# Constant products in TensorE's early waits, and seven block products for eight in the last output projection

## The chip, the core and the metric

The kernel runs on one core of a Trainium2 chip. A core has five engines that work at the same time and wait for each other through semaphores: TensorE (PE: matmuls, reads SBUF, writes PSUM), VectorE (DVE), ScalarE (ACT), GpSimd (POOL) and SyncE (SP, which here only issues transfers). The data memory on the core is SBUF; PSUM holds what matmuls write, in eight banks. The metric is the device time of one execution in microseconds (us); lower is better. Times given for a kernel are the median of several executions. A profile is one further execution, recorded instruction by instruction.

## What is computed

Two layers: a causal attention that looks at chosen chunks of keys only, and a gated feed-forward network on its result. Cut to what matters:

```python
# q, k, v: 4 batches, 8 heads, 768 positions, 64 dims
k_min, k_max = min and max of k over each chunk of 32 positions
ub = sum over d of max(q * k_min, q * k_max)          # for each query and each of 24 chunks
top_chunks = the 6 chunks with the largest ub (chunks in the future excluded)
scores = q @ k.T / 8, where key's chunk is in top_chunks and key <= query, else -1e9
attn = softmax(scores);  x = attn @ v                 # then heads side by side: 3072 x 512

gate = 1 / (1 + exp(-(x @ w_gate)))                   # w_gate, w_val: 512 x 1536
val = x @ w_val
out = (gate * val) @ w_out                            # w_out: 1536 x 512, out: 3072 x 512
```

## The kernel before

**Units.** The 24 blocks of 128 tokens are dealt into eight units u0 to u7 of three blocks (384 tokens; u2 has two blocks and one of the first blocks). Unit u0 holds first blocks of three batches, whose attention is short (`first`). For each other unit the kernel prepares keys and queries (`keys_wide`, `queries_wide`, `keys_blocks`, `queries_blocks`), bounds the chunks and picks the largest six (`choose`: `ub`, `mx`, `ap`, `apt`), and attends (`attend`: scores `sc`, exponentials `exp`, the causal cut `cm` on GpSimd, values `pv`; `finish` divides and transposes the result into the unit's x, `xT`).

**Feed-forward.** Units 0 to 3 go through `ffn`: for each of twelve blocks of 128 of the 1536 hidden columns a gate product `g` and a value product `v` (four matmuls of 384 columns each), `tanh` on ScalarE and the gated product `hg` on VectorE, that is (tanh + 1) * val, with the factor 0.5 applied later. Then `project_out` multiplies with w_out: for each of the three token blocks twelve accumulating matmuls of 512 columns in three quarters of four (`o0`, `o1`, `o2`), an eviction with the factor 0.5 (`osb`), and a transfer out.

**Pairs.** Units 4 and 5, and units 6 and 7, go through `ffn_pair`, which treats the pair's gate (and value) matrix as two by two blocks: the two units by the two halves of the hidden columns, and the two halves of the contraction. It takes seven block products for eight. In each of six rounds f, for the gate (g) and the value (v), TensorE runs the products P1 to P7 of two 384-column matmuls each, into three PSUM tiles; ScalarE or VectorE keep three intermediate states (`E0`, `E1`, `E3`), VectorE adds to them (`C0`, `C1`, `C3`), ScalarE takes the `tanh`, and VectorE makes four gated products `hg_u6u7_x_fb` (unit x of the pair, hidden block fb: f or f + 6). Three of the four read the gate and the kept state, both in SBUF; the fourth, unit 0 with block f + 6, reads its value from PSUM. The sums of weights that it needs (`Sg`, `Sv`) and of tokens (`T`) are made on VectorE. After the rounds, `project_out` runs for the two units as for the others; because each token block's twelve matmuls accumulate over the hidden blocks, its quarters may be taken up as soon as four hidden blocks are ready, in the midst of later rounds. Unit 7's last token block is evicted in two parts (384 and 128 columns).

**Order.** All operations are recorded in a plan with their readers and writers; the order in which they are emitted stands in a table written out in the file, `ORDER`. One word of it names an operation, after @ the engine where it has a choice, and after a colon the numbers of the buffers or PSUM banks that it takes. Each engine works through its operations strictly in this order. The weights come by transfers that GpSimd issues from its own queue (`wg0`, `wv0` and so on: the first third of w_gate, of w_val); they stand behind two small copies (`after0`, `after1`) that wait for early transfers. Queries, keys and values are issued by SP in the table's order.

The lines of the profile that matter here: L501 and L502 issue the weights, L520 and L525 first blocks, L940 is `g` and `v`, L971 the output projection, L980 and L981 its evictions, L1049 the products of a pair, L1064 its additions, L1079 its gated products, L577 the difference of chunk maxima and minima (`kcr`), L874 the causal cut, L349 copies on GpSimd.

Of the kernel before, what the change touches and what calls it, by code (L numbers as in the profile page):

```python
# [11 lines left out]
ALU = mybir.AluOpType  # L12
# [82 lines left out]
vf1_1:0 k1_u1:0 ident q3_u1 ident16 epat0:0 kf1_0:0 tri0 epat qf0_0:1 qf1_0 kf0_0 k2_u2:1 kn_u1_1@POOL:1 hkp011@ACT  # L95
hkp000 kf1_1:2 tri qf0_1:3 kf0_1 v10 scm_0:0,1 hkp001@POOL k3_u2 qf1_1 qfT_0:2 vf_0:4 kfT_0:3 kf0_2:5 qf16_0@DVE:2
kf16_0@DVE:3 vf_1:1 kfT_1:4 kn_u2_2@DVE:4 q2_u2 qn_u1_3@DVE:5 hkf0@DVE kT_u1_1:5 ap0 scf_0:1 hkp110 k0_u1 kt_u1_1:0
expf_0_0 kf1_2 kxf1:0 v16_0_0 expf_0_1:2 qf1_2:0 kcr0 hkp101@POOL kf16_1@DVE:6 qfT_1:6 q3_u2 kx0_u1_1 q1_u2 kx1_u1_1:1
qT_u1_3:7 pvf_0_1:2 pvf_0_0:0 qf0_2 hk1_u1_1@POOL rzf_0_1:0 rzf_0_0:1 q0_u2 kxf0 kT_u2_2:1 vc_1 kn_u1_0:1 q0_u1
xf_0_1:0 qf16_1:2 kT_u1_0:4 hkp010 k0_u2 kt_u2_2:1 scm_1:5,3 k3_u1 xf_0_0:1 hk0_u2_2@ACT vf_2:2 kt_u1_0:2 qf_u1_3:0  # L100
kfT_2:2 scf_1:3 k1_u2 kf16_2:5 qfT_2:6 hq0_u1_3@POOL expf_1_0 k2_u1 scm_2:0,7 hk0_u1_1@POOL qf16_2@DVE:4 expf_1_1:1
q2_u1 after0 pvf_1_0:2 kcr_f@POOL kx0_u2_2 after1 hk0_u1_0@ACT q1_u1 pvf_1_1:5 hk1_u1_0 scf_2:3 qn_u1_0:1 xpsf_0_1:6,0
kx1_u1_0 v_0_1:4 kn_u1_3@POOL:2 hkp111@ACT hkf1@DVE wg0 rzf_1_1:0 rzf_1_0:1 xf_1_0:2 qm_u1_3:0 vf1_2:6 kx0_u1_0
xpsf_0_0:3 wv0 vc_2@ACT xf_1_1:0 expf_2_1:2 xTf_0_0 kn_u1_2@DVE:3 expf_2_0 pvf_2_1:2 kn_u2_1:0 qn_u1_1@POOL:4
pvf_2_0:4 kn_u2_0:5 xpsf_1_1:5 kn_u2_3:6 xTf_1_1 xpsf_1_0:3 hk1_u2_2@ACT rzf_2_1:0 rzf_2_0:1 kx1_u2_2:0 kT_u1_3:7
xTf_0_1 qT_u1_0:0 xf_2_1:1 kt_u1_3:1 kx1_u1_3 hk1_u1_3@POOL qf_u1_0 kT_u2_3:5 xTf_1_0 kT_u1_2:1 qn_u2_3@POOL:2 wv1
kx1_u1_2 wg1 kt_u1_2@DVE:0 xf_2_0:0 hk1_u1_2@ACT v11 kx0_u1_3 qT_u1_1:6 wg2 hq1_u1_0 qf_u1_1@DVE xpsf_2_1:2
qm_u1_0@ACT wv2 kx0_u1_2 kT_u2_0:3 xTf_2_1 kT_u2_1:0 kx1_u2_3 qn_u2_2@POOL:1 kx0_u2_3 wo1 kt_u2_3@DVE:2 qT_u2_3:4
kx0_u2_0 hkp100@POOL kx1_u2_0 kcr_u1 kcr1 kx0_u2_1 qn_u2_1@DVE:6 hq0 hq1 ap1 hk0_u1_2 qf_u2_3@DVE:1 xpsf_2_0:7
# [1122 lines left out]
```

## Time and profile before

| | |
|---|---|
| median of 3 runs | 292.14 us (290.18 to 292.30) |
| the profiled execution | 293.76 us |
| its span, first to last instruction | 292.1 us |
| mean clock granted to TensorE | 0.977 of full |
| TensorE (PE) busy | 274.0 us, 94% |
| VectorE (DVE) busy | 239.4 us, 82% |
| ScalarE (ACT) busy | 211.0 us, 72% |
| GpSimd (POOL) busy | 108.1 us, 37% |

The page gives totals, a row of forty slices for each engine, the chain of work that ended last, and groups of like instructions. Matmuls overlap each other, and their ends are modelled, so busy time of TensorE is not work at its peak; the step from one start to the next says more. An engine that is idle costs nothing by itself: it costs where the engine that sets the end waits for it. The granted clock is the share of full speed that TensorE was given in a stretch.

### The profile page before, as it was taken

What the parts mean: (1) busy time and instruction counts of PE and PEld (TensorE: products, weight loads), DVE (VectorE), ACT (ScalarE), POOL (GpSimd) and SP (SyncE); (2) the same over time, 40 slices, a digit from 0 to 9 for tenths busy, and PEclk for the clock granted to TensorE, in tenths of its full rate; (3) what the DMA queues carried; (4) which work ended last, traced back from release to release, by engine and by line L of the source; (5) the groups of instructions that cost most, each with busy time, mean ns of one, the idle gap of its engine ahead of it and who ended that gap; (6) DMA issues with size and microseconds to landing.
All of it is one profiled execution on the core that took longest, in us unless ns stands there. A gap on an engine that the chain in (4) does not pass through costs nothing.

```text
span 292.1 us, 7079 instructions
## 1 busy us (share of the span) xinstructions
PE 274.0 (94%) x2626; PEld 173.6 (59%) x2626; DVE 239.4 (82%) x653; ACT 211.0 (72%) x450; POOL 108.1 (37%) x176
## 2 busy tenths in 40 slices
PE   2578799999999999999999999999999999999994
PEld 1456366665665666656766656966565565655552
DVE  2959675678999998899999998999998446999840
ACT  3296278769677967886878799999985833996422
POOL 7457325445574335494334577450101110000000
PEclk9977599999999999999999999999999999999999
DMA  6999999989989998969800211100000111000013
GB/s 170 242 272 185 210 222 171 180 172 200 214 170 165 185 207 175 187 129 169 211 2 15 61 39 38 38 1 2 1 2 0 74 72 59 16 0 2 1 72 144
DMA packets 123378, 32.69 MB, mean 112 GB/s; under 512 B 111440, under 2 KB 120400, under 8 KB 123344
## 3 DMA queue, kind: packets, MB, share of 16 engines
q1 hardware_dynamic: 118592, 27.53, 44.2%
q0 software_dynamic: 4752, 4.72, 10.3%
q8 instruction: 20, 0.33, 0.5%
q14 instruction: 14, 0.11, 0.1%
HBM read 30.67 MB, written 6.29 MB: 127 GB/s over the span
## 4 chain that ended last, share of the span: by engine, by line
PE 83%; DVE 5%; DMA 5%; SPq 4%; issue 1%; ACT 1%; POOL 1%; DVEq 0%; ACTq 0%
PE o_u L971 19%; PE sc_u L857 11%; PE v_u L940 11%; PE g_u L940 10%; PE pv_u L890 6%; DMA wv<-in_moe_w_val_dram 3%; PE sug_u6u L1049 3%; PE suv_u6u L1049 3%; PE sug_u4u L1049 3%; PE ube_u L796 3%; PE suv_u4u L1049 2%; SPq L525 2%; SPq L536 2%; PE xps_u L917 2%; PE srv_u4u L1049 1%
## 5 line engine op out<-in xcount | busy, mean ns | idle before, releaser
L868 ACT ACTIVATE att_u<-sc_u 128x512 f16<-128x512 f32 (+3 forms) x184 | 90.1, 557 | 21.0 <-PE sc_u L857 17.1
L874 POOL TENSOR_SCALAR_AFFINE_SELECT att_u<-att_u 128x384 f16<-128x384 f16 (+1 forms) x56 | 29.9, 544 | 79.6 <-ACT att_u L868 69.5
L971 PE MATMUL o_u<-wo,hg_u 128*128 128x512 f16 x216 | 54.1, 379 | 0.0
L940 PE MATMUL v_u<-xT_u,wv 128*128 128x384 f16 x192 | 40.4, 334 | 1.8 <-DMA wv<-in_moe_w_val_dram 1.8
L940 PE MATMUL g_u<-xT_u,wg 128*128 128x384 f16 x192 | 39.7, 330 | 0.0
L948 ACT ACTIVATE gate_u<-g_u 128x384 f16<-128x384 f32 x48 | 23.1, 491 | 10.5 <-PE g_u L940 10.2
L971 PEld LDWEIGHTS <-hg_u 128*128 128x128 f16 x216 | 20.0, 98 | 16.8
L952 DVE SCALAR_TENSOR_TENSOR hg_u<-gate_u,v_u 128x384 f16<-128x384 f16 x48 | 25.0, 534 | 5.3 <-PE v_u L940 3.6
L857 PE MATMUL sc_u<-hqe,hke 128*128 128x128 f16 (+2 forms) x220 | 28.0, 243 | 0.0
L857 PE MATMUL sc_u<-hqo,hko 128*128 128x128 f16 (+2 forms) x220 | 27.6, 243 | 0.1
L890 PEld LDWEIGHTS <-att_u 128*128 128x128 f16 x640 | 24.7, 97 | 4.7 <-issue 0.6
L890 PE MATMUL pv_u<-v,att_u 128*128 128x65 f16 x640 | 26.8, 193 | 0.0
L940 PEld LDWEIGHTS <-wv 128*128 128x128 f16 x192 | 18.4, 100 | 12.6 <-DMA wv<-in_moe_w_val_dram 2.1
L940 PEld LDWEIGHTS <-wg 128*128 128x128 f16 x192 | 18.2, 99 | 10.6 <-issue 1.3
L857 PEld LDWEIGHTS <-hko 128*128 128x128 f16 x220 | 16.7, 98 | 8.5 <-issue 1.7
L857 PEld LDWEIGHTS <-hke 128*128 128x128 f16 x220 | 16.9, 98 | 6.4 <-issue 0.3
L971 PE MATMUL o_u<-wo,hgp_u 128*128 128x512 f16 (+1 forms) x72 | 16.4, 370 | 0.0
L562 POOL CAST v<-v 128x512 f16<-128x512 f32 x23 | 14.9, 660 | 0.7 <-DMA v<-in_v_dram 0.3
L909 DVE TENSOR_TENSOR x_u<-pv_u,rz_u 128x384 f16<-128x384 f32 (+1 forms) x28 | 14.5, 528 | 0.4
L981 DVE TENSOR_SCALAR osb_u<-o_u 128x512 f32<-128x512 f32 x10 | 6.8, 681 | 9.8 <-PE o_u L971 9.6
L980 ACT ACTIVATE osb_u<-o_u 128x512 f32<-128x512 f32 (+1 forms) x14 | 8.1, 589 | 8.6 <-PE o_u L971 8.6
L1049 PEld LDWEIGHTS <-Sv 128*128 128x128 f16 x96 | 9.3, 98 | 6.7 <-issue 0.4
(223 smaller groups left out, 602.4 us busy)
## 6 DMA issues: line engine op xcount, KB each, us to landing
v<-in_v_dram SPq DMA_DIRECT2D x23, 256.0 KB, 4.1
out_dram<-osb_u SPq DMA_DIRECT2D x23, 256.0 KB, 2.0
k<-in_k_dram SPq DMA_DIRECT2D x12, 384.0 KB, 5.9
q<-in_q_dram SPq DMA_DIRECT2D x12, 384.0 KB, 5.3
wg<-in_moe_w_gate_dram POOLq DMA_DIRECT2D x3, 512.0 KB, 10.5
wv<-in_moe_w_val_dram POOLq DMA_DIRECT2D x3, 512.0 KB, 9.7
wo<-in_moe_w_out_dram POOLq DMA_DIRECT2D x3, 512.0 KB, 8.8
kf<-in_k_dram SPq DMA_DIRECT2D x8, 128.0 KB, 3.5
```

Of the source, the lines that this page charges most:

```text
L562: plan.add(f"v16_{b}_{ib}", {POOL: pool(H * D)}, lambda e: nc.gpsimd.tensor_copy(v16[b % 2][:, ib, :, 0:D], at(t)), reads=[t], writes=[("v ...
L796: nc.tensor.matmul(at(ub[e_])[32 * p:32 * p + 32, lo - u.s0:hi - u.s0], kcr[par][ROWS[e_], p, m, :], at(src)[ROWS[e_], p, lo:hi], start=(m ...
L857: nc.tensor.matmul(at(t)[:, o:o + 128 * m], hk[b % 2][e_][:, p, 128 * jb:128 * jb + 128], hq[u.side][e_][:, p, 128 * x:128 * (x + m)], sta ...
L868: plan.add(f"exp_{u.name}_{h}_{y}", {ACT: act(n)}, lambda e, t=t, att=att, b0=b0, n=n: nc.scalar.activation(at(att)[:, b0:b0 + n], at(t), ...
L874: nc.gpsimd.affine_select(out=dv, in_=dv, compare_op=ALU.is_ge, fill=0.0, base=0, pattern=[[0, u.m], [1, 128]], channel_multiplier=-1)
L890: nc.tensor.matmul(at(pv)[:, last, x, :], at(att)[:, c:c + 128], v16[b % 2][:, jb, h, :], start=(jb == 0), stop=(jb == ib))
L909: plan.add(f"x_{u.name}_{p}", {DVE: dve(u.t)}, lambda e: nc.vector.tensor_tensor(at(x_).rearrange("p a (e d) -> p e a d", e=2), at(pv)[:, ...
L940: nc.tensor.matmul(at(t), w16[:, c, 128 * fb:128 * fb + 128], at(u.xt)[:, c, :], start=(c == 0), stop=(c == 3))
L948: plan.add(f"tanh_{u.name}_{fb}", {ACT: act(T)}, lambda e, g=g, gate=gate: nc.scalar.activation(at(gate), at(g), AF.Tanh, scale=0.5), read ...
L952: plan.add(f"hg_{u.name}_{fb}", {DVE: dve(T)}, lambda e, w_=w_, gate=gate, hg=hg: nc.vector.scalar_tensor_tensor(at(hg), at(gate), 1.0, at ...
L971: nc.tensor.matmul(at(o), hgs[c][1][1]()[:, 128 * tb:128 * tb + 128], wo16[:, fc, lo:hi], start=(c == 0), stop=(c == NFB - 1))
L1049: nc.tensor.matmul(at(t), left[i](c), right[i](c), start=first and c == 0, stop=c == 1, skip_group_check=not first)
```

## The change

**Constant products.** Thirty matmuls `wm_0` to `wm_29` are added to the plan. Each multiplies the 128x128 identity with itself four times side by side (512 columns) into a PSUM bank that nobody reads. They wait only for the identity and for their bank. The table places them one by one among TensorE's operations: 27 before the first gate product of unit 0, and `wm_7`, `wm_27` and `wm_12` behind it, among unit 0's feed-forward and unit 1's attention.

**The last pair's output projection.** For units 6 and 7 a new function `project_pair` takes the place of two calls of `project_out`. It treats the two units' gated products as two by two blocks (unit, half of the hidden columns) and w_out as two by two blocks (half of the hidden columns, half of the 512 output columns), and forms the four output blocks from seven block products. For this it needs sums:

- `So0` to `So3`, for each of six f: sums of gated products, 128x384 f16 (So0 = unit 7's two halves added, So1 = So0 less unit 6's first half, So2 = unit 6's first half less unit 7's, So3 = unit 6's second half less So1). They may run on VectorE or GpSimd; the table gives 20 of the 24 to GpSimd.
- `To0` to `To3`: differences of blocks of w_out, 128x1536 f16; the table gives all four to GpSimd, To2 in the stage of units 4 and 5, To0 and To1 within the rounds of units 6 and 7, To3 behind them.

Then for each of three token blocks TensorE runs seven products of six 256-column matmuls, into three PSUM tiles; `E0`, `E1`, `E3` keep intermediate states (times 0.5), and `D0` to `D3` write the four output blocks. The sums lie in buffers that held keys and queries of attention.

**The table** is drawn anew: every operation has another place in it, and some have another engine.

The diff without the table, cut to its core:

```diff
+        for f in range(half):
+            a11, a12, a21, a22 = a(0, f), a(0, f + half), a(1, f), a(1, f + half)
...
+            for i, x, op, y, need in ((0, a21, ALU.add, a22, [k21, k22]), (1, lambda f=f: s_(0, f), ALU.subtract, a11, [("so", 0, f), k11]),
+                                      (2, a11, ALU.subtract, a21, [k11, k21]), (3, a12, ALU.subtract, lambda f=f: s_(1, f), [k12, ("so", 1, f)])):
...
+                plan.add(f"So{i}_{tag}_{f}", {DVE: dve(T, 2), POOL: pool(1.6 * T)}, lambda e, i=i, f=f, x=x, op=op, y=y: (
+                    nc.vector if e == DVE else nc.gpsimd).tensor_tensor(s_(i, f), x(), y(), op),
+                    reads=need, writes=[("so", i, f)] + place[room][1], port=True, prio=next_(EV))
...
+        for i, x, op, y, need in ((0, b12, ALU.subtract, b11, []), (1, b22, ALU.subtract, lambda: t_(0), [("to", 0)]),
+                                  (2, b22, ALU.subtract, b12, []), (3, b21, ALU.subtract, lambda: t_(1), [("to", 1)])):
+            plan.add(f"To{i}_{tag}", {DVE: dve(1536, 2), POOL: pool(1.6 * 1536)}, lambda e, i=i, x=x, op=op, y=y: (
+                nc.vector if e == DVE else nc.gpsimd).tensor_tensor(t_(i), x(), y(), op),
+                reads=wos_ + need, writes=[("to", i)] + [(k_, 0, *z) for k_, z in every(0, i // 2)], port=True, prio=next_(EV) - 1)
+        left = {1: lambda f: a(0, f)(), 2: lambda f: a(0, f + half)(), 3: lambda f: s_(3, f), 4: lambda f: a(1, f + half)(),
+                5: lambda f: s_(0, f), 6: lambda f: s_(1, f), 7: lambda f: s_(2, f)}
+        right = {1: lambda f: wo16[:, f, 0:w], 2: lambda f: wo16[:, half + f, 0:w], 3: lambda f: wo16[:, half + f, w:2 * w],
+                 4: lambda f: t_(3, f), 5: lambda f: t_(0, f), 6: lambda f: t_(1, f), 7: lambda f: t_(2, f)}
...
+            op = mul(1, u_, True)
...
+            keep_(0, u_)
+            mul(2, q_, True)
+            done(0, q_)
+            mul(5, r_, True)
+            keep_(3, r_)
+            mul(6, u_, False)
+            keep_(1, u_)
+            mul(3, r_, False)
+            done(1, r_)
+            mul(7, u_, False)
+            done(3, u_)
+            mul(4, u_, False)
+            done(2, u_)
...
+        if ub_ is units[7]:
+            project_pair(ua, ub_, hg, next_)
+            return
         for x, u in ((0, ua), (1, ub_)):
             project_out(u, [(fb, hg[x, fb]) for f in range(half) for fb in (f, f + half)], [], next_)
...
+    for i in range(30):
+        w = ps(f"wm_{i}", "wm", [128, 4, 128])
+        plan.add(f"wm_{i}", pe(512 / 2.4 + 2.4), lambda e, w=w: nc.tensor.matmul(
+            at(w), ident16, ident16.unsqueeze(1).to_broadcast([128, 4, 128]), start=True, stop=True),
+            reads=["ident16"], writes=[w], prio=-2.0 + 0.1 * i)
```

The end of the new table, from the last round on, shows where the sums stand:

```
So3_u6u7_2@POOL E3v_u6u7_5:0 P2v_u6u7_5 C0g_u6u7_5 E1g_u6u7_5:4 P6v_u6u7_5 C0v_u6u7_5 So2_u6u7_3@POOL P7g_u6u7_5
E1v_u6u7_5:3 C3v_u6u7_4 So3_u6u7_3@POOL tanh_u6u7_0_5:1 P7v_u6u7_5 C3g_u6u7_5 P4v_u6u7_4 C3v_u6u7_5 P4g_u6u7_5
hg_u6u7_0_5 P4v_u6u7_5 tanh_u6u7_0_11:1 P3v_u6u7_5 hg_u6u7_0_10 hg_u6u7_0_11 tanh_u6u7_1_11:2 hg_u6u7_1_10 C1g_u6u7_5
P1o_u6u7_1:6,1,2,3,2 P2o_u6u7_0:0 So0_u6u7_4@POOL C1v_u6u7_5 P1o_u6u7_0:7,4,0,1 tanh_u6u7_1_5:3 So1_u6u7_4@POOL
hg_u6u7_1_11 E0o_u6u7_1:6 E0o_u6u7_0:5 hg_u6u7_1_5 So0_u6u7_5 So1_u6u7_5 So3_u6u7_4 So2_u6u7_4 So3_u6u7_5@POOL
```

More of the change, by code (lines that the diff above doesn't have):

```diff
@@ L94 @@
 ORDER = """
[L95 to L109, printed above, removed]
@@ new lines @@
+kn_u2_2@POOL:2 expf_1_1:1 rzf_0_0:0 kt_u1_0@DVE:1 q3_u2 wm_25:0 hq0_u1_3@POOL scm_2:0,5 expf_1_0 xf_0_0:0 k1_u2 wg0
+kx1_u1_0:1 pvf_0_1:6 kf16_2:3 wm_24:1 k3_u2 xpsf_0_0:1,0 kx0_u1_3 wm_5:3 vc_1@ACT qT_u1_1:3 v11 k0_u2 xTf_0_0 wm_6:2
+hk1_u1_0 kT_u2_2:2 qf_u1_1 vf1_3:4 pvf_1_0:7 kcr_f@POOL kT_u1_2:1 vc_2 rzf_1_0:0 kx1_u1_3 scf_2:2 wm_15:3 rzf_0_1:1
+wv0 expf_2_0 wm_10:3 hq1 xf_0_1:1 pvf_1_1:3 expf_2_1:3 xf_1_0:2 pvf_2_0:4 qn_u2_0@POOL:2 wm_19:0 rzf_1_1:0
+kt_u2_2@DVE:2 kn_u2_1:6 wm_17:0 hkp110@POOL xf_1_1:0 pvf_2_1:0 xpsf_1_0:6 rzf_2_0:0 xTf_1_0@ACT xpsf_0_1:7 rzf_2_1:1
```

406 lines of the change are left out of this document (243 added, 163 removed).

## The prediction

> **What bounds the kernel now.** I read the page from the top: engine totals and the slices first.
>
> ```profile
> span 292.1 us, 7079 instructions
> PE 274.0 (94%) x2626; PEld 173.6 (59%) x2626; DVE 239.4 (82%) x653; ACT 211.0 (72%) x450; POOL 108.1 (37%) x176
> PEclk9977599999999999999999999999999999999999
> ```
>
> TensorE (PE) is busy nearly throughout, so shares say little; what counts is which stretch has TensorE at full rate and which does not. So next the busy time by stretches, cut where the work changes (columns: stretch, its length, then busy us and instructions of PE, weight loads, DVE, ACT, POOL, then the granted clock, DMA share, GB/s).
>
> ```profile
> 30.90:36.40 5.50, 5.50 (x36) 2.29 (x44) 3.07 (x9) 0.49 (x1) 0.76 (x2) 0.50 1.39 214
> 187.00:217.00 30.00, 29.88 (x270) 19.47 (x268) 29.51 (x64) 28.15 (x67) 7.10 (x12) 1.00 0.01 2
> 217.00:245.50 28.50, 28.40 (x259) 16.84 (x256) 16.97 (x38) 15.83 (x34) 3.03 (x6) 1.00 0.10 39
> 245.50:280.40 34.90, 34.86 (x207) 19.94 (x206) 31.99 (x66) 23.57 (x55) 0.00 (x0) 1.00 0.04 16
> 280.40:288.30 7.90, 7.87 (x44) 3.69 (x42) 0.69 (x2) 2.18 (x5) 0.00 (x0) 1.00 0.40 155
> 288.30:292.10 3.80, 0.00 (x0) 0.00 (x0) 0.00 (x0) 0.60 (x1) 0.00 (x0) 1.00 0.25 91
> ```
>
> Three things are to be seen. In the first row TensorE works 5.5 us at a clock of 0.50. In the fourth, the last feed-forward pair (units 6 and 7), TensorE is full but VectorE (DVE) has only 2.9 us to spare, and GpSimd (POOL) does nothing at all: 0.00 (x0). In the fifth, after the last gated product, TensorE alone runs for 7.9 us on output projections.
>
> **The start: thirty constant products.** Each is one 128x512 matmul. Twenty-seven stand in TensorE's queue ahead of the first gate product g_u0_0, three behind it.
>
> ```profile
> 13.00:16.40 3.40, 1.53 (x15) 1.16 (x16) 2.13 (x7) 2.06 (x6) 2.15 (x3) 0.98 1.00 249
> 16.40:19.70 3.30, 2.96 (x28) 2.01 (x26) 1.39 (x4) 3.30 (x7) 1.51 (x6) 0.50 0.96 265
> 19.70:23.10 3.40, 1.89 (x29) 1.43 (x26) 3.32 (x12) 3.34 (x8) 2.20 (x5) 1.00 1.07 277
> 26.50:29.90 3.40, 1.59 (x11) 0.86 (x10) 3.40 (x10) 2.75 (x8) 3.36 (x6) 1.00 1.21 188
> 29.90:33.20 3.30, 2.31 (x8) 1.14 (x9) 3.05 (x9) 0.90 (x3) 1.70 (x3) 0.50 1.31 209
> ```
>
> Cut this way the clock follows the stretch before it: after TensorE was busy 1.53 of 3.40 the next stretch has 0.50, after 2.96 of 3.30 it has 1.00, after 1.89 and 1.59 of 3.40 again 0.50, and 2.31 of 3.30 did not yet bring it back. The 5.5 us at half clock from 30.9 therefore hold 2.75 us of loss, and filling the waits can win that much. It wins the full amount only if the wait for the value weights is filled too:
>
> ```profile
> 30.89 1.46 PE L940 MATMUL v_u<-xT_u,wv 128*128 128x384 f16 x4 [1.76 <-DMA wv<-in_moe_w_val_dram]
> 20.11 0.99 POOL wg L501
> 21.15 9.69 DMA wv<-in_moe_w_val_dram
> 7.56 0.51 SPq L520 DMA_DIRECT2D vf<-in_v_dram  x1
> 16.22 0.41 SPq L520 DMA_DIRECT2D vf<-in_v_dram  x1
> vf<-in_v_dram SPq DMA_DIRECT2D x4, 256.0 KB, 3.8
> ```
>
> The first value product started when that transfer landed, 9.69 us after its issue. In the new table GpSimd issues wg0 behind v16_0_0, hkp001 (a 1.46 us copy, row below), kn_u2_2 and hq0_u1_3, and wv0 behind vc_2, which needs the nineteenth and the twenty-sixth load of SP. By the pace of SP before (the two rows are its thirteenth and twenty-seventh load; 3.8 us to landing) I work out some 19 us for wg0 and 21 to 22 for wv0: no earlier landing, so FFN 0 starts at about 31 us as before. Behind g_u0_0 the new order has two more transposes (about 0.4 us each) and three constant products (0.22 each at the full rate below). Start: -2.75 + 0.8 + 0.65 = **-1.3 us**; from -4 (transfer 2.7 us earlier) to +1.5 (clock as before, the added products paid).
>
> **The out-projection of the last pair.** Rates from the chain of waits:
>
> ```profile
> 232.54 1.73 PE o_u L971 x8
> 248.26 0.65 PE sug_u6u L1049 x4
> ```
>
> A 512-wide product takes 0.216 us, a 384-wide one 0.163. Before, units 6 and 7 need the columns of 72 such 512-wide products, 15.6 us. After, 21 block products of six 256-wide matmuls: 126 x 0.109 = 13.7 us (0.109 is half of 0.216). TensorE: **-1.8 us**. But every block product needs the gated products of all six rounds, so none can run inside the pair's stage, where 8.2 us of them ran before. There TensorE now has 82 pair products of two 384-wide matmuls (26.7 us) and one leftover quarter of unit 5 (0.9), VectorE 62 operations. Their pace:
>
> ```profile
> 260.37 0.55 DVE L1064 TENSOR_TENSOR c0g_u6u<-c0g_u6u,sqg_u6u 128x384 f32<-128x384 f32 x1
> 260.84 0.55 DVE L1064 TENSOR_TENSOR c1g_u6u<-c1g_u6u,srg_u6u 128x384 f32<-128x384 f32 x1
> 261.30 0.55 DVE L1064 TENSOR_TENSOR c3g_u6u<-c3g_u6u,sug_u6u 128x384 f32<-128x384 f32 x1
> ```
>
> One starts every 0.47 us: 62 x 0.47 = 29.1. So VectorE is the bound of this stage, without slack, where TensorE was. With 1.5 us at its beginning the last gated product is 30.6 us behind the stage's first product (34.9 before); then the first product on the last sums starts 0.9 later and sixteen products of 0.65 end the kernel: 42.0 against 34.9 + 7.9 = 42.8. With the 0.9 us of unit 5 moved in from before the stage this is the -1.8 again, if nothing else waits. The last eviction is 256 wide in place of 512 (0.60 below): **-0.15 us**.
>
> ```profile
> 286.38 1.89 PE L971 MATMUL o_u<-wo,hgp_u 128*128 128x512 f16 x8
> 288.30 0.60 ACT L980 ACTIVATE osb_u<-o_u 128x512 f32<-128x512 f32 x1 [1.45 <-PE o_u L971]
> ```
>
> **The sums on GpSimd.** The block products need 24 sums of gated products (So, 128x384) and four of weights (To, 128x1536), each of two operands in SBUF; the table gives 20 So and all To to GpSimd. The trace before has no such size there. The nearest rows:
>
> ```profile
> L577 POOL TENSOR_TENSOR kcr<-kx_f,kcr x1: 208/208/208, 17.9 to 17.9; 128x16 f32<-128x16 f32 x1
> L577 POOL TENSOR_TENSOR kcr<-kx_u,kcr x1: 263/263/263, 46.3 to 46.3; 128x32 f32<-128x32 f32 x1
> L577 POOL TENSOR_TENSOR kcr<-kx,kcr x1: 382/382/382, 86.1 to 86.1; 128x96 f32<-128x96 f32 x1
> L349 POOL COPY hke<-kt_u 64x384 f16<-64x384 f16 x1 | 0.5, 501 | 0.0
> L349 POOL COPY hke<-epat 64x1536 f16<-64x1536 f16 x3 | 4.4, 1461 | 0.2
> ```
>
> From 32 to 96 elements an element costs 1.86 ns, from 16 to 96 2.18. Carried on: So 0.92 to 1.01, To 3.06 to 3.51. The copies, with one operand, are the lower end: 0.50 and 1.46. I take 0.97 and 3.3, the rows of the same operation.
>
> What they cost others is in the older pair's rows:
>
> ```profile
> 214.92 0.55 DVE L1079 SCALAR_TENSOR_TENSOR hgp_u<-gate_u4u,c3v_u4u 128x384 f16<-128x384 f16 x1
> 215.39 0.87 DVE L1079 SCALAR_TENSOR_TENSOR hg_u<-gate_u4u,c0v_u4u 128x384 f16<-128x384 f16 x1
> 215.23 0.62 POOL L874 TENSOR_SCALAR_AFFINE_SELECT att_u<-att_u 128x384 f16<-128x384 f16 x1 [7.43 <-ACT att_u L868]
> 207.40 0.83 DVE L1079 SCALAR_TENSOR_TENSOR hgp_u<-gate_u4u,c3v_u4u 128x384 f16<-128x384 f16 x1
> 206.99 0.82 POOL L349 COPY hqo<-apt_u 64x768 f16<-64x768 f16 x1
> ```
>
> A gated product that reads gate and value from SBUF takes 0.55, but 0.87 and 0.83 when GpSimd is at work as it starts; both end 0.41 us after GpSimd's operation (215.85 and 207.81). It waits for the whole of it. In each round of the pair three of the four gated products are of this kind (the fourth reads PSUM). Before, GpSimd idled in this stage. The Trainium skill says the same in "SBUF — State Buffer", section "Who interferes with whom": a VectorE instruction with two SBUF inputs contends with a GpSimd one that reads SBUF, and the later is blocked fully; here the trace agrees (0.87 for 0.55).
>
> I walked the new table's two queues side by side from So0_0 on: 47 VectorE operations, 22 us, against 16 So and two To, 22 us: GpSimd is never ahead, so it is mostly at work when one of the 15 gated products of this kind comes up. To0 starts 1.1 us in and runs to 4.4; hg_1_1 arrives at 1.4 and waits 2.9. To1 runs 8.75 to 12.05; hg_0_2 arrives at 9.2 and waits 2.8. Nine others wait 0.1 to 0.95 for So, 5.2 together. VectorE being the bound, this adds **+10.9 us**; by the copies' prices the same walk gives 2.8. To2 stands in the stage of units 4 and 5, where VectorE is busy 29.51 of 30.00: one gated product arrives some 1.5 us into its 3.3, **+1.8** (0 to 3). So3, So2 and To3 behind the last round end about when their products come up: 0.
>
> The rest of the table, 36 to 187 us, is drawn anew over the same work: 0, give or take 1.5.
>
> **Sum**: -1.3 - 1.8 - 0.15 + 10.9 + 1.8 = +9.45 us. The profiled execution took 293.76 (span 292.1 and 1.66 around it), 1.6 above the median of the runs, 292.14. On that median: 301.6.
>
> **The rivals.**
> *Short sums.* GpSimd takes f16 sums at its copies' price: waits 2.8 + 0.8 instead of 12.7, sum +0.35, 292.5 us. For it: the rows of sums are f32 and small. Against: its copies cost the same in f32 and f16.
> *No meeting*, the one on the faster side: GpSimd's sums do not hold VectorE up, say because the wait falls into time that VectorE spends on the evictions of ScalarE. Place: the last pair; price: the 12.7 away, -3.25, 288.9 us. It decides as soon as all waits are below 3.25, a So of about 0.5. Against it stand the 0.87 and 0.83 and the 29.1 of VectorE over 27.6 of TensorE.
> *The clock falls in the last stage.* With 27.6 us of products in some 41, TensorE is busy 67%; stretches of 47 and 56% above were followed by 0.50, one of 70% did not restore it. Two such stretches at half rate would cost some 4 us: 305.5. The Trainium skill ("TensorE: Matmul & The Clock Gate", Part 1) lets the clock fall only after a whole idle window, about 3.4 us; by that rule this rival is void. Here the trace differs: it fell after 1.89 busy of 3.40.
> *The start does not warm*: the change doesn't do what it says. TensorE still waits for the value weights just before 31 us, and the stretch before is too empty: start +0.65, 303.5.
>
> **How the numbers follow.** Forecast as summed 0.50, no warm start 0.08, falling clock 0.12 (all slower); short sums 0.17; no meeting 0.13. One per cent, 2.9 us, is about what a measurement tells from no change here (the three runs lie 2.1 apart). Slower by more: 0.68, with 0.02 of the slower cases within; within: 0.19; faster: 0.13. The range leaves out no meeting and the far part of the falling clock: 291.5 to 306.5.
>
> **What would show it.** Right: in the last pair, gated products of over 1 us on VectorE that end 0.4 us behind a GpSimd sum; a stage of some 41 us from its first product to the last gated one; So near 1 us, To over 3; clock 1.00 from 31 us. Wrong: gated products at 0.55 throughout, So at 0.5, the last stage under 32 us, or a first value product well ahead of 30 us.

## The result and the profile after

The changed kernel took 302.22 us (median of four runs, 302.0 to 304.58) against 292.06 us for the kernel before on the same chip: a ratio of 1.038, with a 95% interval of 1.031 to 1.045. It is slower by some 10 us. Forecast were 301.6 us.

The page of the changed kernel: span, engine totals, granted TensorE clock in 40 slices. Both profiled executions lie above their kernels' medians, this one (304.58 us, the longest of the four) by 2.4 us and the one before (293.76 us) by 1.7.

```profile
span 302.7 us, 7259 instructions
PE 280.7 (93%) x2698; PEld 178.2 (59%) x2698; DVE 249.7 (83%) x655; ACT 210.7 (70%) x450; POOL 153.4 (51%) x216
PEclk9979999999999999999999999999999999999999
```

GpSimd (POOL) has 45 us more than before. The clock is at full rate from 20 us on, where before the half rate came back at 31 us. The same execution by stretches, with the prediction's columns (length, then busy us and instructions of PE, weight loads, DVE, ACT, POOL, granted clock, DMA share, GB/s), cut where this kernel's work changes:

```profile
30.90:36.40 5.50, 4.72 (x29) 2.65 (x29) 4.74 (x14) 1.38 (x4) 4.65 (x6) 1.00 1.19 189
187.00:217.00 30.00, 28.24 (x268) 18.60 (x266) 29.62 (x60) 27.87 (x65) 10.96 (x12) 1.00 0.01 1
217.00:248.63 31.63, 31.41 (x302) 19.08 (x300) 21.37 (x47) 18.38 (x40) 4.09 (x7) 1.00 0.09 36
248.63:288.21 39.58, 33.76 (x204) 19.66 (x202) 37.72 (x62) 25.26 (x59) 24.12 (x20) 1.00 0.04 13
288.21:299.00 10.79, 10.37 (x92) 8.81 (x91) 6.84 (x17) 1.92 (x5) 5.01 (x3) 1.00 0.26 99
299.00:302.70 3.70, 0.01 (x1) 0.00 (x0) 0.42 (x1) 0.00 (x0) 0.00 (x0) 0.96 0.37 142
```

The last pair's stage (248.63 to the end of the last gated product) takes 39.6 us for 34.9 before. TensorE waits 5.8 us in it and VectorE is busy 37.7 with 62 operations: the bound has passed from TensorE to VectorE. The stretch behind it takes 10.8 us for 7.9. The stage begins 3.1 us later than before (248.63 against 245.49). These three make up the difference of the two spans: 4.7 + 2.9 + 3.1 = 10.7, and 10.6 are measured.

Why VectorE is busy so long is seen in the order of time. First GpSimd's queue, then VectorE's, from the last stage of the changed kernel (start, duration, engine, line, operation, out<-in):

```profile
258.14 0.92 POOL L1026 TENSOR_TENSOR hke<-hgp_u 128x384 f16<-128x384 f16 x1 [15.30 <-DVE hgp_u L1199]
259.01 3.09 POOL L1040 TENSOR_TENSOR hke<-wo 128x1536 f16<-128x1536 f16 x1
...
265.54 3.40 POOL L1040 TENSOR_TENSOR hke<-wo,hke 128x1536 f16<-128x1536 f16 x1
```

```profile
258.98 0.55 DVE L1184 TENSOR_TENSOR c3v_u6u<-c3v_u6u,suv_u6u 128x384 f32<-128x384 f32 x1
259.44 3.08 DVE L1199 SCALAR_TENSOR_TENSOR hgp_u<-gate_u6u,c1v_u6u 128x384 f16<-128x384 f16 x1
...
265.91 0.54 DVE L1184 TENSOR_TENSOR c0g_u6u<-c0g_u6u,sqg_u6u 128x384 f32<-128x384 f32 x1
266.38 2.98 DVE L1199 SCALAR_TENSOR_TENSOR hg_u<-gate_u6u,c0v_u6u 128x384 f16<-128x384 f16 x1
```

To0 runs from 259.01 to 262.10; the gated product that comes up in that time takes 3.08 and ends at 262.52. To1 ends at 268.94; the product that came up at 266.38 ends at 269.36. Both end 0.42 us behind GpSimd. An addition that reads PSUM (265.91), which comes up while To1 runs, takes its usual 0.54.

### The profile page after: what moved, and what is told of

Its sections match the earlier page's. It is cut to its first block, busy times and chain, and to the rows that moved or that the text cites. A ratio compares the mean times of both kernels' runs of the same rounds, so it can differ in the third digit from the quotient of the medians.

```text
span 302.7 us, 7259 instructions
## 1 busy us (share of the span) xinstructions
PE 280.7 (93%) x2698; PEld 178.2 (59%) x2698; DVE 249.7 (83%) x655; ACT 210.7 (70%) x450; POOL 153.4 (51%) x216
## 5 line engine op out<-in xcount | busy, mean ns | idle before, releaser
L979 PE MATMUL o_u<-wo,hg_u 128*128 128x512 f16 x180 | 43.9, 379 | 0.0
L948 PE MATMUL v_u<-xT_u,wv 128*128 128x384 f16 x192 | 39.0, 326 | 0.1
L865 PE MATMUL sc_u<-hqe,hke 128*128 128x128 f16 (+2 forms) x220 | 28.4, 243 | 1.3 <-DVE c1g_u4u L1184 1.3
L865 PE MATMUL sc_u<-hqo,hko 128*128 128x128 f16 (+2 forms) x220 | 28.9, 243 | 0.1
L898 PE MATMUL pv_u<-v,att_u 128*128 128x65 f16 x640 | 27.6, 193 | 0.5 <-DVE c0g_u4u L1184 0.4
L979 PEld LDWEIGHTS <-hg_u 128*128 128x128 f16 x180 | 16.7, 98 | 15.2
L948 PEld LDWEIGHTS <-wv 128*128 128x128 f16 x192 | 18.2, 98 | 10.6 <-issue 0.3
L1026 POOL TENSOR_TENSOR hke<-hgp_u 128x384 f16<-128x384 f16 x5 | 4.6, 914 | 20.7 <-DVE hgp_u L1199 20.7
L1259 PE MATMUL wm<-ident 128*128 128x512 f16 x30 | 12.4, 415 | 0.6
```

The lines of the kernel that those rows point to most:

```text
L865: nc.tensor.matmul(at(t)[:, o:o + 128 * m], hk[b % 2][e_][:, p, 128 * jb:128 * jb + 128], hq[u.side][e_][:, p, 128 * x:128 * (x + m)], sta ...
L898: nc.tensor.matmul(at(pv)[:, last, x, :], at(att)[:, c:c + 128], v16[b % 2][:, jb, h, :], start=(jb == 0), stop=(jb == ib))
L948: nc.tensor.matmul(at(t), w16[:, c, 128 * fb:128 * fb + 128], at(u.xt)[:, c, :], start=(c == 0), stop=(c == 3))
L979: nc.tensor.matmul(at(o), hgs[c][1][1]()[:, 128 * tb:128 * tb + 128], wo16[:, fc, lo:hi], start=(c == 0), stop=(c == NFB - 1))
L1259: plan.add(f"wm_{i}", pe(512 / 2.4 + 2.4), lambda e, w=w: nc.tensor.matmul(at(w), ident16, ident16.unsqueeze(1).to_broadcast([128, 4, 128] ...
```

## The experiments

Each kernel is the changed one with the edit shown. The "held time" counts, over all gated products longer than 0.65 us, what is above 0.54 us for each. In the changed kernel it is 8.2 us in the last stage and 3.1 in the stage of units 4 and 5; in the kernel before it is 0 and 0.6. The ratios are to the kernel before on the same chip. The runs were made on more than one chip, so the difference of two times and the difference of their ratios do not agree to better than about 1 us.

**No constant products, and all sums on VectorE.**

```
-    for i in range(30):
+    for i in range(0):
...
-(thirty words wm_*)
```

> The changed kernel without its thirty constant products, everything else in its order. In its trace a constant product takes 0.43 us from start to start, not the 0.22 of the forecast, so the 27 ahead of the first gate product hold TensorE for 11.6 us and the queue ahead of g_u0_0 is busy nearly without a gap until 34.5 us. Theory A (they fill TensorE's in-order queue and delay its start): g_u0_0 starts at 29 to 32 us, and the time falls by 1.5 to 4 us, to 298 to 300.5 us. Rival (they stand in waits and keep the clock up): g_u0_0 starts where it did, the granted clock falls to 0.5 around it, and the time is the same or rises by up to 3 us, 302 to 305 us.

Measured: 299.16 us, 1.025 (1.017 to 1.033), so some 3 us less than the changed kernel (nearly 4 by the ratios). The start of this kernel, TensorE's queue and GpSimd's issue of the first value weights:

```profile
26.89 0.65 PE L699 MATMUL kT_u<-ident,kn_u 128*128 128x128 f32 x3 [1.33 <-DVE kn_u L351]
27.33 1.48 PE L944 MATMUL g_u<-xT_u,wg 128*128 128x384 f16 x4
29.45 1.37 PE L944 MATMUL v_u<-xT_u,wv 128*128 128x384 f16 x4 [0.64 <-DMA wv<-in_moe_w_val_dram]
```

```profile
20.80 0.80 POOL L506 DMA_DIRECT2D wv<-in_moe_w_val_dram  x1
```

and the same places in the changed kernel:

```profile
33.22 0.44 PE L703 MATMUL qT_u<-ident,qn_u 128*128 128x128 f32 x2
34.12 0.55 PE L703 MATMUL kT_u<-ident,kn_u 128*128 128x128 f32 x3 [0.46 <-DVE kn_u L355]
34.50 0.81 PE L948 MATMUL g_u<-xT_u,wg 128*128 128x384 f16 x4
```

```profile
26.70 0.80 POOL L510 DMA_DIRECT2D wv<-in_moe_w_val_dram  x1
```

Theory A holds: without the constant products the first gate product starts at 27.3 us for 34.5, earlier even than the 29 to 32 expected, though at half rate at first. With them even the issue of the value weights on GpSimd, which has no constant product in its queue, comes 5.9 us later: what TensorE's queue delays, the engines behind it pass on.

```
-So0_u6u7_0@POOL ... To0_u6u7@POOL ...
+So0_u6u7_0@DVE  ... To0_u6u7@DVE  ...      (all 24)
```

> The changed kernel with all 24 sums of the last pair's projection (So and To) on VectorE. Theory A (GpSimd's sums hold VectorE's gated products): the lengthened gated products go, 8.1 us in the last stage and 1.8 in the stage of units 4 and 5; VectorE pays some 14 sums So of 0.27 us and three sums To of 0.9 ahead of its last gated product, 6.4 us. The time is 297.5 us (296 to 299.5), with no gated product over 0.7 us in the last stage. Rival (the loss lies in the projection standing behind the stage and in the table, whichever engine takes the sums): VectorE's stage is only longer by the sums, the time is 302 to 308 us.

Measured: 299.78 us, 1.027 (1.019 to 1.035). This is 0.3 above the range for theory A and 2 below the rival's. No gated product of the last stage is over 0.7 us. The stage of this kernel:

```profile
247.19:285.10 37.91, 33.60 (x202) 19.54 (x201) 36.05 (x82) 25.39 (x59) 0.00 (x0) 1.00 0.04 14
```

GpSimd does nothing in it and VectorE does 82 operations for 62. Forming the sums on VectorE costs the stage nearly what the waits had cost: 37.9 for 39.6 us.

**Three weight sums early on GpSimd; fills in place of sums.**

```
-... To2_u6u7@POOL (stage of units 4, 5) ... To0_u6u7@POOL ... To1_u6u7@POOL (last stage)
+... o0_u4_0 To2_u6u7@POOL ... hg_u4u5_0_11 To0_u6u7@POOL ... sc_u7_5_3 To1_u6u7@POOL
```

> The changed kernel with three of the four weight sums (To0, To1, To2) still on GpSimd, but in the stretch between the stages of the two pairs, where VectorE has few gated products. Theory A: the gated products of 3.08 and 2.98 us in the last stage and the one of 2.36 in the stage of units 4 and 5 become 0.55, which is 6.8 us less on VectorE; the sums So keep their 2.9 us of waits. The time is 295.5 us (294.5 to 297.5). Rival (the stage is lost elsewhere and these waits are covered): 301 to 303 us.

Measured: 300.49 us, 1.030 (1.021 to 1.039). Theory A's number was missed by 5 us. The two queues show why; GpSimd, then VectorE:

```profile
216.43 3.09 POOL L1038 TENSOR_TENSOR hko<-wo 128x1536 f16<-128x1536 f16 x1
219.48 3.41 POOL L1038 TENSOR_TENSOR hke<-wo 128x1536 f16<-128x1536 f16 x1
```

```profile
217.20 2.74 DVE L1197 SCALAR_TENSOR_TENSOR hgp_u<-gate_u4u,c3v_u4u 128x384 f16<-128x384 f16 x1
...
221.32 1.98 DVE L1197 SCALAR_TENSOR_TENSOR hgp_u<-gate_u4u,c1v_u4u 128x384 f16<-128x384 f16 x1
```

A place in the table orders an engine's own queue only. GpSimd had nothing ahead of these sums and ran them from 216 us on, in the middle of the gated products of units 4 and 5. The held time fell from 11.3 to 8.8 us, by 2.5, and the time by 1.7: the theory stands, the edit did not do what I meant.

```
-    nc.gpsimd.tensor_tensor(s_(i, f), x(), y(), op)
+    o, x, y = s_(i, f), x(), y()
+    nc.gpsimd.tensor_tensor(o[:, 0:8], x[:, 0:8], y[:, 0:8], op)
+    for _ in range(2): nc.gpsimd.memset(o[:, 8:T], 0.0)
...
-    nc.gpsimd.tensor_tensor(t_(i), x(), y(), op)
+    for _ in range(2): nc.gpsimd.memset(t_(i), 0.0)
```

> The changed kernel with each sum on GpSimd replaced by work of like length that reads next to nothing: of a sum So only the first 8 columns are formed, and two fills of the whole width follow; a weight sum To becomes two fills of its room. The sums, and so the outputs of the last pair, are left out. Theory A in its narrow form (it is GpSimd's reading of two SBUF tensors that VectorE's gated products wait for): no gated product is over 0.7 us, and the time falls by 8 to 11 us, to 291 to 294 us. Rival (any long work on GpSimd holds them, or they wait for GpSimd's data): gated products stay at 1 to 3 us while the fills run, 300 to 303 us.

Measured: 294.19 us, 1.014 (1.010 to 1.018), 8 us below the changed kernel (7 by the ratios) and 0.2 above the range of theory A. GpSimd, then VectorE, then the stage and the stretch behind it:

```profile
254.24 0.88 POOL L1012 MEMSET hke<- 128x376 f16 x2
255.06 2.81 POOL L1016 MEMSET hke<- 128x1536 f16 x2
```

```profile
255.39 0.55 DVE L1206 SCALAR_TENSOR_TENSOR hgp_u<-gate_u6u,c1v_u6u 128x384 f16<-128x384 f16 x1
...
257.44 0.55 DVE L1206 SCALAR_TENSOR_TENSOR hgp_u<-gate_u6u,c3v_u6u 128x384 f16<-128x384 f16 x1
```

```profile
244.58:276.35 31.77, 31.61 (x197) 19.11 (x196) 29.90 (x62) 24.68 (x59) 21.22 (x52) 1.00 0.04 17
276.35:288.10 11.75, 11.14 (x100) 9.39 (x98) 6.21 (x17) 1.92 (x5) 6.81 (x15) 1.00 0.23 90
```

This is the run that decides. The first gated product is the very one that took 3.08 us in the changed kernel; here it comes up 0.33 us into fills of 2.81 us and takes 0.55. GpSimd is busy 21.2 us of the stage, and not one product of it is held. So neither GpSimd's being at work nor its writing into SBUF holds VectorE; its sums, which read two SBUF tensors, do. In the prediction's rows a causal cut and a copy, which read one, held a product too (0.87 and 0.83). The stage falls from 39.6 to 31.8 us, by 7.8, for 8.2 us of held time in it. The stretch behind it grows by 1.0, from 10.8 to 11.75, so of the 8.2 us held 6.9 are won in the two together. The Trainium skill ("SBUF — State Buffer", section "Who interferes with whom") says of a VectorE instruction with two SBUF inputs that it contends with a GpSimd instruction that reads SBUF and not with one that only writes it: the trace agrees on both halves, 3.08 us beside the sum and 0.55 beside the fill. A fill differs from a sum in its instruction too, so that it is the reading and not the operation is the nearest explanation rather than a proof; that cuts, copies and sums all hold, and fills alone do not, speaks for it.

**The width and the data of a constant product.**

```
-    w = ps(f"wm_{i}", "wm", [128, 4, 128])      ... to_broadcast([128, 4, 128])
+    w = ps(f"wm_{i}", "wm", [128, 2, 128])      ... to_broadcast([128, 2, 128])
```

> The changed kernel with its thirty constant products 256 wide in place of 512. If a constant product's 0.43 us scales with its width, the 27 ahead of g_u0_0 take 5.8 us less of TensorE's queue: theory A (they delay the start) expects g_u0_0 at 28 to 31 us with the clock kept up, and a time 2 to 4 us below the changed kernel's, 298 to 300 us, no worse than without any constant product (299.16). Rival (an instruction costs 0.43 us whatever its width, or the start waits for its transfers): within 1 us of the changed kernel, 301 to 303 us.

```
-    nc.tensor.matmul(at(w), ident16, ident16.unsqueeze(1)...
+    nc.tensor.matmul(at(w), ident16, tri.unsqueeze(1)...
```

> The changed kernel with the mask tile in place of the identity as the moving side of its constant products (weights: the identity, as before); their outputs are read by nobody in either kernel. The two mask products of a block, of the same shape, stand 0.21 us apart in the trace, the constant products 0.43. If the doubled time comes from the identity being both the weights and the moving side, the pitch falls to 0.21 and the time by 1.5 to 4 us, to 298 to 300.5 us. If it belongs to a product that ends its own group in one instruction, the pitch stays 0.43 and the time 301 to 303 us.

Measured: half the width 300.8 us, 1.029 (1.021 to 1.038); the mask tile 303.89 us, 1.041 (1.035 to 1.048). Three constant products in a row in the changed kernel, at half the width, and with the mask tile (three rows from three traces, in this order):

```profile
29.84 1.24 PE L1259 MATMUL wm<-ident 128*128 128x512 f16 x3
```

```profile
28.20 0.92 PE L1258 MATMUL wm<-ident 128*128 128x256 f16 x3
```

```profile
29.61 1.24 PE L1258 MATMUL wm<-tri,ident 128*128 128x512 f16 x3
```

One alone lasts 0.38 at full width and 0.27 at half, so the pitch is (1.24 - 0.38) / 2 = 0.43 and (0.92 - 0.27) / 2 = 0.32 us. Half the width saves 0.11, which is 256 columns at the rate of the out-projections; some 0.21 us of each stay at both widths. Both pitches are the duration and 0.05 us more: what follows a constant product starts when that has ended by the trace (whose ends of products are modelled), while a chain of out-projections overlaps. My first idea, that the identity on both sides doubles it, falls: with the mask tile the pitch is the same. What makes the next product wait stays open. Neither time met its range. With half the width g_u0_0 came at 32.6 us, not at 28 to 31, because the clock in that execution was at 0.50 from 14 to 20 us, and the time lies between the two cases; with the mask tile it is 0.9 above the range, g_u0_0 at 34.3 us after a clock of about 0.7 in the same place.

**The weight sums on VectorE between the stages; no constant products with the fills.**

```
-To0..To3 on GpSimd, in the stages and behind the last
+hg_u4u5_0_11 To0@DVE ... osb_u4_1 To1@DVE ... osb_u4_2 To2@DVE ... hg_u4u5_1_10 To3@DVE
```

> The changed kernel with the four weight sums (To) on VectorE, in the stretch between the two pairs' stages (0.9 us each, where VectorE is busy 21.4 of 31.7 us); the 20 sums So stay on GpSimd. The run with three of them early on GpSimd had its waits moved into the stage of units 4 and 5, since nothing held GpSimd back. Theory A (each us that a gated product is held is lost at the end): the products of 3.08, 2.98 and 2.36 us become 0.55 and no others grow, -6.8 us, with the four sums hidden in VectorE's slack; the time is 295.5 us (294.5 to 297.5). Rival (the stretch has no slack for 3.6 us of VectorE, or only part of the held time counts): 298 to 301 us.

Measured: 297.6 us, 1.020 (1.013 to 1.027), 0.1 above the range for theory A. The two products of 3.08 and 2.98 us are 1.09 and 1.08 here, not 0.55: with the weight sums out of its queue GpSimd forms the sums So earlier, and these now meet the same products. The held time of the last stage is 4.1 us, for 3.2 from the sums So before. Its stage, with GpSimd busy 17.5 us:

```profile
244.57:280.18 35.61, 33.31 (x204) 19.67 (x202) 33.55 (x62) 25.14 (x59) 17.47 (x18) 1.00 0.04 15
```

The stage stands 3.8 us above that with fills: this is the price of the sums So alone.

```
+fills in place of the sums (as above)
-the thirty constant products (as above)
```

> The changed kernel without its constant products and with each sum on GpSimd replaced by fills of like length (of a sum So only 8 columns are formed; the sums, and so the outputs of the last pair, are left out). What stays of the change: the seven block products behind the stage and the redrawn table. If the two effects add, -3.0 and -8.0 us on the changed kernel: 291 us (290 to 292.5), as long as the kernel before. By the forecast's terms without the sums' waits, the time would be 288.5 to 290.5 us: then the effects don't add but the product's saving of 1.8 us is there. Over 292.5 us, the table or the products' place behind the stage costs something of its own.

Measured: 291.76 us, 0.999 (0.995 to 1.002). The two effects add up to the whole of the loss: without the sums' reading and without the constant products the rest of the change, seven block products and a new table, is neither a gain nor a loss to within 0.5%.

**Putting it together.** Six constant products alone; then six, with the weight sums on VectorE and either all or seven of the sums So there as well; then ten, with the weight sums and six sums So on VectorE.

```
-    for i in range(30):
+    for i in (4, 8, 9, 16, 20, 26):
```

> The changed kernel with six of its thirty constant products, those that stand last ahead of g_u0_0 (4, 8, 9, 16, 20, 26). Without any, g_u0_0 came at 27.3 us with TensorE waiting 1.2 and 1.3 us just ahead of it, and the first three feed-forward products ran at half the rate. Theory A (constant products are worth what they put into a wait and cost 0.43 us of the queue elsewhere): the six fill the last two waits, g_u0_0 starts at 27.5 to 28.5 us at the full clock, and the time is 0.5 to 2 us below the kernel without constant products (299.16), 297 to 298.8 us. Rival (the clock needs all of them, or the start then waits for the value weights): 299 to 301 us.

> The changed kernel with these three edits together: six constant products, the four weight sums on VectorE between the stages, and all 20 sums So on VectorE. No sum is left on GpSimd, so no gated product of the last stage is held; VectorE pays some 14 sums of 0.27 us ahead of the last gated product, 3.8 us. From the run with all sums on VectorE (299.8): -2.7 us for the weight sums moved out of the stages and -3 to -4.5 for the start, 292.5 to 294.5 us, at best as long as the kernel before. Below 292 us the single gains would add up to more than they were alone; over 295.5 the sums So cost more than their 0.27 us.

> As the run with six constant products and all sums on VectorE, but of the 20 sums So only the seven that held a gated product longest in the trace of the run with the weight sums moved (So1 of rounds 0, 1, 3, 4, So3 of 0 and 1, So2 of 2) are on VectorE; the others stay on GpSimd. VectorE pays 7 x 0.27 = 1.9 us and is to be rid of 3.6 us of holding: from that run (297.6) -1.7 and -3 to -4.5 for the start, 291.5 to 293 us. Rival (any sum on GpSimd holds whichever two-SBUF operation of VectorE comes next, the seven sums now among them): the holding only moves, 293.5 to 295 us.

> As the mixed run (292.86 us), with ten constant products for six (10, 15, 17 and 19 more, which stand between 20 and 23 us) and So3 of round 1 back on GpSimd, since on VectorE it was itself held to 1.06 us. In the mixed run's trace TensorE waited 1.6 us between 19.5 and 22.3 us, and the granted clock was 0.50 from 23 to 28.4 us. If the four products fill those waits and the clock stays at 1.00, g_u0_0 starts at 27.5 to 29 us for 29.2 and the time is 291.3 to 292.3 us. If their 0.43 us each only lengthen the queue, or the start then waits for the value weights, the time is 292.6 to 294 us.

| run | time | ratio to the kernel before | g_u0_0 | last stage |
|---|---|---|---|---|
| six constant products | 298.51 | 1.022 (1.016 to 1.028) | 29.4 | 39.6 |
| six, all sums on VectorE | 294.34 | 1.008 (1.005 to 1.010) | 27.6 | 36.3 |
| six, weight sums and seven So on VectorE | 292.86 | 1.002 (1.000 to 1.005) | 29.2 | 35.2 |
| ten, weight sums and six So on VectorE | 292.29 | 1.001 (0.997 to 1.004) | 28.4 | 35.0 |

All four times are within the ranges expected of the edits, the last at its upper end. Of the details two were missed: with six products alone g_u0_0 came at 29.4 us, not at 28.5 or before, for the clock fell to 0.50 ahead of it; with ten it stayed at 1.00, as expected, and the time is 0.6 us less, which the intervals of the two ratios do not separate. The last kernel's ratio can't be told from 1. In the mixed run one sum on VectorE met a sum on GpSimd and was itself held, at 1.06 us for 0.36:

```profile
267.75 1.22 POOL L1022 TENSOR_TENSOR hko<-hg_u,hgp_u 128x384 f16<-128x384 f16 x1
```

```profile
268.13 1.06 DVE L1022 TENSOR_TENSOR hko<-hke,hg_u 128x384 f16<-128x384 f16 x1
```

The best version takes back all of the 10 us, but it does not beat the kernel before: its sums still cost the stage 3.2 us over the fills (35.0 for 31.8).

## Why the prediction was right

The forecast of 301.6 us and its sign were right, and its main term was the largest cause. Three terms of the sum were off: the waits were taken too long, and the start and the out-projection too short.

**The sums' durations.** Taken were 0.97 for a So and 3.3 for a To, from rows of the same operation at smaller sizes. Two groups of the changed kernel (count, then busy us and mean ns):

```profile
L1026 POOL TENSOR_TENSOR hko<-hg_u,hgp_u 128x384 f16<-128x384 f16 x4 | 3.6, 912 | 0.0
L1040 POOL TENSOR_TENSOR hko<-wo 128x1536 f16<-128x1536 f16 x1 | 3.1, 3095 | 0.0
```

They are 0.91 and 3.1 undisturbed, and up to 1.23 and 3.4 where a sum itself had to wait for VectorE. The rival of short sums, by the copies' 0.50 and 1.46, is void.

**The waits in the last stage.** Forecast +10.9 us; by the rows 8.2 us, by the stage with fills 7.8, and with the stretch behind it 6.9. To0 and To1 hold as forecast, a little less (2.5 and 2.4 us for 2.9 and 2.8), and the seven products lengthened by the So 3.2 us in all, for 5.2. The walk along the two queues kept GpSimd at work without a gap from So0_0 on; in the trace it was busy 24.1 of the 30.1 us from there to the last gated product, and in between waited itself for VectorE's products. This term was too large by 3 to 4 us.

**To2 among units 4 and 5.** Forecast +1.8 us. One gated product takes 2.36 us there, 1.8 above its 0.55, and ends 0.41 behind the sum. With fills the way from this pair's first product to the last stage is 1.8 us shorter (184.43 to 244.58 us, for 186.67 to 248.63), so the whole wait is paid there. First GpSimd's row, then VectorE's:

```profile
210.58 3.10 POOL L1040 TENSOR_TENSOR hko<-wo 128x1536 f16<-128x1536 f16 x1
```

```profile
211.73 2.36 DVE L1199 SCALAR_TENSOR_TENSOR hgp_u<-gate_u4u,c1v_u4u 128x384 f16<-128x384 f16 x1
```

**The stage and the out-projection without waits.** Forecast: 30.6 us to the last gated product, set by VectorE, and 11.3 behind it (0.9 and sixteen products of 0.65), in all 0.8 less than before. With fills, where no product is held, the two take 31.8 and 11.75 us: 43.5 for the 42.8 before, a loss of 0.7. The premise that none of the projection can run inside the stage was wrong. The products P1 and P2 read unit 6's gated products alone and need not wait for unit 7's last. With fills 28 of the projection's 126 matmuls lie inside the stage; in the changed kernel, where TensorE has waits to fill, 35 do, and the stretch behind takes 10.8. Two rows of the changed kernel, ahead of the stage's end at 288.21:

```profile
284.31 0.82 PE L1060 MATMUL suo_u6u<-wo,hg_u 128*128 128x256 f16 x6
286.28 1.47 PE L1060 MATMUL sqo_u6u<-wo,hg_u 128*128 128x256 f16 x12
```

That VectorE bounds the stage holds with the waits in it (37.7 busy of 39.6 us, TensorE 33.8). Without them TensorE is busy 31.6 of 31.8 us and VectorE 29.9, so there it is not shown.

**The start.** This term failed: "-1.3", with FFN 0 at 31 us as before and the constant products at 0.22 each. A constant product takes 0.43, and the 27 ahead of g_u0_0 take 11.6 us of TensorE's queue, more than its waits hold. They keep the clock up but push the start to 32.2 to 34.5 us; without any of them it is 27.3. Their cost is 3 to 4 us (299.16 against 302.22 us; ratios 1.025 and 1.038). The clock was not safe with them either: in the profiled execution it fell once more,

```profile
14.00:17.00 3.00, 2.83 (x19) 1.53 (x16) 1.66 (x4) 2.35 (x5) 1.84 (x3) 0.79 0.86 230
17.00:20.00 3.00, 2.89 (x14) 1.43 (x12) 1.32 (x3) 0.00 (x0) 0.77 (x3) 0.65 1.08 260
```

and g_u0_0 came at 34.5 us. In three runs with the same thirty products (the weight sums moved early, the weight sums on VectorE, and the fills) the clock stayed at 1.00 there and g_u0_0 came at 32.2. My own mark for "wrong", a first value product well ahead of 30 us, came nowhere: with all thirty at full width it starts at 32.9 to 35.2 us, and the earliest starts are 29.4 with ten and 29.5 without any.

**The rest of the table.** Forecast 0, give or take 1.5. It is not small, but it cancels: the table moved work over the boundary at unit 4's pair. From the first feed-forward product to that pair, and from there to the last pair, first before, then after:

```profile
28.31:190.32 162.01, 159.91 (x1785) 103.57 (x1784) 144.74 (x444) 127.92 (x268) 82.03 (x128) 0.98 0.77 143
190.32:245.49 55.17, 54.95 (x472) 33.69 (x471) 43.27 (x93) 40.66 (x92) 8.54 (x15) 1.00 0.06 20
```

```profile
34.50:188.10 153.60, 153.42 (x1715) 100.22 (x1713) 136.96 (x425) 126.63 (x265) 90.36 (x137) 1.00 0.78 149
188.10:248.63 60.53, 58.55 (x549) 36.74 (x547) 49.93 (x103) 45.15 (x101) 15.05 (x19) 1.00 0.05 19
```

TensorE has 70 instructions less in the first stretch and 77 more in the second, and the first holds 6.5 us less of TensorE's time, part of it the half clock of before.

**The balance.** The runs give the sum in three parts. Without the held products and without constant products the kernel takes as long as before (ratio 0.999), where the forecast's terms give -1.2 us (-1.8 - 0.15 + 0.8). The constant products cost 3 to 4 us, where the forecast has them win 2.1 (-2.75 + 0.65). The sums on GpSimd cost 7 to 8 us, where the forecast has 12.7 (10.9 + 1.8). So the waits were taken some 5 us too long, and the start and the projection together 6 to 7 us too short. The mechanism of the main term was right; that the totals agree so closely is luck.

By stretches of the profiled executions: forecast was that the last stage begins 0.4 us earlier (-1.3 + 1.8 - 0.9) and that everything from there takes 9.9 us longer (-0.9 - 0.15 + 10.9). It began 3.1 us later and took 7.6 longer (39.6 + 10.8 against 42.8). Some 2.3 of the 3.1 us go with the clock's fall at the start, by the 32.2 us of the three runs in which it stayed up. The three shorter executions of the changed kernel, with spans of 300.3 to 300.4 us, may lack these 2.3 us, but no trace of them shows it, and one of them has a mean clock as low as the profiled one's (0.993 for 0.994).

**The rivals.** *No meeting* would have left the products at 0.55; they were up to 3.08. With the fills the waits are gone and the time is 294.2 us, not the rival's 288.9: its price, 12.7 us, was some 5 too large. *The clock falls in the last stage* did not come: TensorE was busy 33.8 of 39.6 us, 85%, where the rival had 67% by counting only the steps between the pair's products, and the clock stayed at 1.00. The rule of the Trainium skill by which that rival was void ("TensorE: Matmul & The Clock Gate", Part 1: the clock falls only after a whole idle window, about 3.4 us) agrees with this stage; with the start it does not, as the last section shows. *The start does not warm*: the clock was warm at the start, and the start was late all the same, by another mechanism than the rival's.

## What to carry to other kernels

Work given to GpSimd beside a VectorE-bound stage has a second price beside its own duration: each VectorE operation with two SBUF inputs that comes up meanwhile waits for the rest of it. Look first at what GpSimd's operation reads; a fill was free here, a sum of two SBUF tensors was not, and in the changed kernel two sums of 3 us held VectorE for 5.0 us, and the eighteen of 0.9 to 1.2 beside them for 3.2.

Products that only keep the clock up stand in an in-order queue: price them by their measured pitch, put them only where the queue waits anyway, and count what the engines behind TensorE then get later. And where a table decides the places, a place orders one engine's queue and nothing else.

## What the runs showed of the hardware that was not expected

- A 512-wide constant product, alone in its group, takes 0.43 us from start to start at a granted clock of 1.00; a 512-wide out-projection product takes 0.216. At 256 columns it is 0.32, so some 0.21 us come on top of the columns at both widths. With the mask tile on the moving side the pitch is the same.
- GpSimd's fills of 2 x 1536 columns (2.81 us) hold no gated product of VectorE, while a sum of like length holds one for 2.5 us.
- The holding goes both ways: a So on GpSimd takes 0.91 alone and 1.23 where it met a gated product, and a So on VectorE 0.36 alone and 1.06 where it met GpSimd's.
- The clock fell without any long idle time. With six constant products alone TensorE's longest wait between 13 and 23 us was 0.68 us, and yet the granted clock was 0.50 from 23 us on; with ten it stayed at 1.00. Rows of the two, in this order:

```profile
23.00:28.50 5.50, 5.09 (x17) 1.85 (x16) 3.53 (x13) 0.98 (x3) 5.46 (x8) 0.50 1.15 187
```

```profile
23.00:26.00 3.00, 2.63 (x18) 1.11 (x17) 2.71 (x10) 0.65 (x2) 3.00 (x6) 1.00 1.21 226
```

In the execution with six constant products and all sums on VectorE the clock stayed at 1.00 up to 29 us, with less work of TensorE ahead: busy 1.82 and 2.11 us of 17 to 20 and 20 to 23 us, where the run with six alone had 1.90 and 2.30:

```profile
17.00:20.00 3.00, 1.82 (x22) 1.39 (x21) 1.89 (x5) 1.83 (x4) 2.69 (x7) 1.00 1.06 259
20.00:23.00 3.00, 2.11 (x34) 1.42 (x33) 2.58 (x11) 1.95 (x5) 2.93 (x4) 1.00 0.98 166
```

So neither the longest wait nor the busy share of the stretch before tells when the clock falls, and the prediction's reading that the clock follows the stretch before it does not hold here. What makes it fall stays open.
